# Weights prepared once for two pairs of token blocks, two of four sums kept in PSUM, and the float64 conversion in the room of a used input

## Chip, cores and metric

One NeuronCore of a Trainium2 chip runs the whole program. The metric is the time of one execution on the device in microseconds (us); of several timed runs the median counts.

## What is computed

Three layers follow one another on 2304 tokens:

```python
# 1: linear attention, 4 batches x 8 heads, 576 tokens, head width 64
proj = x @ w_phi                                  # 64 -> 128 features, for q and for k
proj = proj - max(abs(proj))
phi = concat(exp(proj), exp(-proj))
x = (phi(q) @ (phi(k).T @ v)) / (phi(q) @ sum(phi(k)) + 1e-6)
# 2: four experts, all used for every token, x is 2304 x 512
for e in range(4):
    out += p[:, e:e+1] * (relu(x @ w1[e]) @ w2[e])   # 512 -> 1024 -> 512
# 3: gated layer
y = (((x @ v1) * (x @ v2)) @ w3) @ w_out             # v1, v2: 512 -> 1024
```

The weights of the third layer (v1, v2, w3, w_out) arrive as float64, the rest as float32. Every matrix product of the layers 2 and 3 is made in three passes on split operands: each operand is written as a rounded high part and the low rest, and high x high, high x low and low x high are added.

## The kernel before

**Tokens and visits.** The tokens form six blocks of 384 (`TB`), used in pairs of 768 (`PW`): layer 2 sees pairs 0, 1, 2, layer 3 the same tokens as pairs 3, 4, 5. The hidden width of the four experts is cut into 16 columns of 256. A *visit* (list `visits`, L668 to L674) is one column of weights for one pair: the up-products, the relu and the down-products of that column. In order: 11 `plain` visits (columns 0 to 7 of pair 0, the products made directly, between the heads of the attention), 8 `expert` visits (columns 8 to 15 of pair 0), 16 for pair 1, then for each of 16 columns a `fold` (a part of w3 @ w_out, which makes one matrix of the two last ones) and an `expert` visit for pair 2, and 24 for layer 3: for each pair and each of 4 columns a `gate` (x @ v1) and a `gated` visit (x @ v2, the product of both, and the down-product).

**The up-products.** From the `expert` visits on they follow a Strassen-like scheme with 7 products in place of 8 (`strassen_up`, L732). It needs seven combinations of the weight quarters and seven of the input's quarters (`quarter_tasks`, L635: subtractions and splits on VectorE and ScalarE). The products go to three PSUM banks a, b, c of a pool of five (`mmb`). Three intermediate states of a are copied to SBUF by ScalarE (`out_of`, L740: tiles `s`), and VectorE adds banks to them (`plus`, L747), the sum staying in the SBUF tile. Four results come out, three in SBUF, one in bank a. `relu` (L773) turns each into h: ScalarE writes the high part, VectorE the low one.

**The down-products.** Six per visit (`down`, L783), each 6 matmuls of 512 columns into one of three other banks (`mma`); VectorE multiplies each by the token's share and adds it to its accumulator `acc` in SBUF (L812), of which one set of six serves one pair at a time.

**Weights.** Each visit prepares its own weights (`prefetch`, L684): a load of 512 KB on the queue of SyncE (SP) into a staging tile `raw` (two buffers), and then the splits and sums. `strassen_tasks` (L296): the split of 768 columns of raw (ScalarE casts, VectorE in the experts or POOL in the gates subtracts, L277), four sums of 256 columns on POOL (L311, tile `sm`), and the split of those 1024. The second weight is one cast and one subtraction of 1024 columns (POOL in experts and gates, VectorE in folds).

**float64.** [...] `nearest_tasks` (L321) reads the two halves of each number as integers: a load (`cr`), one ScalarE operation to `cf`, five on VectorE between `cf` and `ct`, and a store of the float32 result to DRAM (`near`). There are 40 halves (w_out 8, w3 16, v1 8, v2 8); each `expert` visit of pair 0 puts two of them into the work, each other one. The tiles cr, cf, ct have one buffer each, in a pool `cv` of their own.

**What sets the order.** `Prog.run` (L118) plans the program with given costs of each operation: an operation runs when its inputs are there and its tiles have room, the smallest number (turn of the visit, then order of writing) first. What comes out is the fixed order of each engine and of SP's queue. Side work (preparations, conversions, quarters) lies in a list `bg` and is written out piece by piece by `work()` after steps of the visit, the rest by `drain()`. The step `phase_c` (L971) waits for the whole attention, closes its pools and opens those of the transformed products; `phase_s` (L980) waits until the input of pair 0 (`xr0`) is used, closes it and opens `st`, the pool of the tiles s. All products of `strassen_up` wait for it (`after=start["S"]`). The inputs of the later pairs lie in a pool `xr` of two buffers.

Of the kernel before, what the change touches and what calls it, by code (L numbers as in the profile page):

```python
# [24 lines left out]
TB = 384  # L25
# [12 lines left out]
KA = 8  # L38
# [18 lines left out]


class Value:


    def __init__(self, prog, pool, shape, dt, tag, bufs, name):
        self.prog, self.args, self.key = prog, (shape, dt, tag, bufs, name), (pool, tag)
        self.tile, self.writers, self.readers, self.left, self.live = None, [], [], 0, False
# [4 lines left out]
    def __call__(self):  # L69
# [3 lines left out]
        return self.tile  # L73

# [7 lines left out]
class Prog:  # L82
# [15 lines left out]
    def op(self, eng, ns, fn, reads=(), writes=(), fills=(), after=(), prio=None, wait=0.0):  # L98
# [13 lines left out]
        o.values = list({id(v): v for v in (*reads, *writes, *fills)}.values())  # L112
# [79 lines left out]
def fused_kernel(ctx, tc, qT, kT, vt, w_phi, probs, w1, w2, v1, v2, w3T, w_out, out):  # L192
# [12 lines left out]
    pools["stage"] = ec(tc.tile_pool(name="stage", bufs=2))  # L205
# [62 lines left out]
    def gp(n):  # L268
        return n * 2.45 + 10

    def split_ops(raw, hi, lo, n, w, eng, after=()):

        e, ns = (nc.gpsimd, gp(n)) if eng == POOL else (nc.vector, dve(n))
# [8 lines left out]
    def load_piece(src, nm, reads, after, n=4):  # L282
        raw = V("stage", [128, n, 256], F32, "raw", 2, f"raw_{nm}")
# [37 lines left out]
    def nearest_tasks(src, key, i, h):  # L321

        nm = f"{key}{i}_{h}"
        raw = V("cv", [128, 512, 2], I32, "cr", 1, f"cr_{nm}")
        f = V("cv", [128, 512], F32, "cf", 1, f"cf_{nm}")
        t = V("cv", [128, 512], F32, "ct", 1, f"ct_{nm}")
# [3 lines left out]
                out=raw().rearrange("p c w -> p (c w)"), in_=src.bitcast(I32)[:, h * 1024:h * 1024 + 1024]  # L330
            ), 1 << 19, writes=[raw], after=start["C"]),
            lambda: op(ACT, act(n) + 90, lambda: nc.scalar.mul(
                f(), raw()[:, :, 1].bitcast(F32), 2.0 ** -112
            ), reads=[raw], writes=[f]),
            lambda: op(DVE, 430, lambda: v.tensor_scalar(
# [6 lines left out]
            lambda: op(DVE, 430, lambda: v.tensor_scalar(  # L342
# [3 lines left out]
                out=t(), in0=raw()[:, :, 0].bitcast(U32), scalar=2.0 ** -52, in1=t(), op0=ALU.mult, op1=ALU.mult  # L346
# [271 lines left out]

    quarters = {}

    def quarter(i, q):

        if (i, q) not in quarters:
            pool, bufs = ("xc", 7) if i % 2 else ("xs", 4) if q[0] == "B" else ("xt", 4)
            quarters[i, q] = V(pool, [128, 2, 2, TB], F32R, "q", bufs, f"x{i}_{q}")
# [42 lines left out]
    visits = [("plain", c, 0, (0,)) for c in range(EB)] + [("plain", c, 0, (1,)) for c in range(EB)]  # L668
# [385 lines left out]
```

## Time and profile before

| | us |
|---|---|
| median of 3 runs | 1436.79 (1435.93 to 1442.55) |
| the profiled execution | 1438.74 |
| its span | 1436.9 |

| engine | busy us | share of the span | instructions |
|---|---|---|---|
| TensorE matmul (PE) | 1328.6 | 92% | 6739 |
| TensorE weight load (PEld) | 1175.0 | 82% | 6739 |
| VectorE (DVE) | 1097.1 | 76% | 1553 |
| ScalarE (ACT) | 678.9 | 47% | 1266 |
| GpSimd (POOL) | 652.9 | 45% | 472 |

The busy times are sums over the whole span, and stages with different limits lie in it. Matmuls are pipelined and their ends are modelled, so a busy PE is not PE at its peak. In rows, the names are those of the program without buffer numbers: `h<-s,h` writes h from s and h. Idle time stands with what ended it.

### The profile page before, as it was taken

Reading aid. Unit: us, or ns where it says so; the run is one execution under the profiler, and the core shown is the slowest. Engines: PE = TensorE matmul, PEld = TensorE weight load, DVE = VectorE, ACT = ScalarE, POOL = GpSimd, SP = SyncE. Lnnn points to the kernel's source line nnn. Section 1 sums busy time; section 2 is a strip of 40 time slices with the busy share of each in tenths; the row PEclk is TensorE's granted clock in tenths of the full one; section 3 lists DMA queues with packets and bytes.
Section 4 is the critical chain, followed back from the end, with each engine's and each line's share of the span. In section 5 each row is a group of like instructions: output and inputs, shape, how many; then the busy total and the mean of one; then the engine's idle time right before and its main releaser. Section 6 shows DMA issues by size and latency. Waiting matters only on the chain.

```text
span 1436.9 us, 18521 instructions
## 1 busy us (share of the span) xinstructions
PE 1328.6 (92%) x6739; PEld 1175.0 (82%) x6739; DVE 1097.1 (76%) x1553; ACT 678.9 (47%) x1266; POOL 652.9 (45%) x472
## 2 busy tenths in 40 slices
PE   8889999999889888888979999998999999999998
PEld 7778888988777777777868778887888888889997
DVE  5678987979988988789887986667666475776665
ACT  5768866854333343333333443443443554454451
POOL 3333322304534435344543433534444758758780
PEclk8989999999999999999999999999999999999999
DMA  5554443223334244341443343332232312222311
GB/s 142 135 154 117 131 137 103 67 70 100 103 114 136 90 130 124 103 123 58 135 125 117 128 129 105 107 104 88 96 110 96 90 43 88 74 76 86 117 59 45
DMA packets 79372, 149.38 MB, mean 104 GB/s; under 512 B 33425, under 2 KB 37905, under 8 KB 79281
## 3 DMA queue, kind: packets, MB, share of 16 engines
q1 hardware_dynamic: 79280, 148.20, 33.6%
q8 instruction: 53, 0.87, 0.3%
q14 instruction: 39, 0.31, 0.1%
HBM read 130.72 MB, written 17.45 MB: 103 GB/s over the span
## 4 chain that ended last, share of the span: by engine, by line
PE 41%; DVE 34%; DMA 10%; issue 6%; ACT 6%; POOL 2%; SPq 0%; ACTq 0%; DVEq 0%; POOLq 0%
PE dn L789 15%; PE upa L720 10%; PE upb L720 5%; DVE acc L812 4%; DVE h L777 4%; PE psw L862 3%; DVE w_a L277 2%; PE upc L720 2%; DMA near_w<-cf_w 2%; PE kvp L485 2%; DMA rb<-rd 2%; DVE s L748 2%; DVE w_b L277 2%; DVE xsum L651 2%; PE num L574 2%
## 5 line engine op out<-in xcount | busy, mean ns | idle before, releaser
L789 PE MATMUL dn<-w_b,h 128*128 128x512 f32 x1728 | 433.7, 399 | 17.7 <-DVE acc L812 15.0
L789 PEld LDWEIGHTS dn<-w_b,h 128*128 128x128 f32 x1728 | 326.1, 191 | 86.3 <-DVE acc L812 19.7
L720 PE MATMUL upa<-x_T,w_a 128*128 128x384 f32 x1152 | 247.5, 351 | 54.9 <-ACT s L742 54.5
L720 PEld LDWEIGHTS upa<-x_T,w_a 128*128 128x128 f32 x1152 | 209.2, 194 | 80.6 <-ACT s L742 74.6
L311 POOL TENSOR_TENSOR sm_a<-raw_a 128x256 f32<-128x256 f32 x128 | 111.5, 871 | 287.9 <-DMA raw_a<-w 211.6
L812 DVE SCALAR_TENSOR_TENSOR acc<-dn,pn,acc 128x512 f32<-128x512 f32 x270 | 197.1, 743 | 42.6 <-PE dn L789 42.3
L277 POOL TENSOR_TENSOR w_a<-sm_a,w_a 128x1024 fp32r<-128x1024 f32 x64 | 163.1, 2549 | 79.1 <-ACT w_a L275 79.1
L277 POOL TENSOR_TENSOR w_b<-raw_b,w_b 128x1024 fp32r<-128x1024 f32 x52 | 132.9, 2555 | 131.5 <-ACT w_b L275 131.5
L550 POOL PARTITION_ALL_REDUCE M<-Ps x64 | 87.1, 1366 | 203.4 <-ACT Ps L547 182.1
L742 ACT COPY s<-upa 128x384 f32<-128x384 f32 x192 | 91.1, 475 | 114.7 <-PE upa L720 114.6
L775 ACT ACTIVATE h<-s 128x384 fp32r<-128x384 f32 x120 | 62.7, 523 | 157.1 <-DVE s L748 153.9
L748 DVE TENSOR_TENSOR s<-upb,s 128x384 f32<-128x384 f32 x128 | 70.7, 552 | 75.3 <-ACT s L742 47.2
L275 ACT CAST w_b<-raw_b 128x1024 fp32r<-128x1024 f32 x79 | 83.0, 1051 | 94.5 <-PE dn L789 60.1
L777 DVE SCALAR_TENSOR_TENSOR h<-s,h 128x384 fp32r<-128x384 f32 x120 | 96.1, 801 | 19.6 <-ACT h L775 19.5
L789 PE MATMUL dn<-w_b,g 128*128 128x512 f32 x432 | 106.8, 396 | 0.0
L277 DVE TENSOR_TENSOR w_a<-raw_a,w_a 128x768 fp32r<-128x768 f32 (+1 forms) x67 | 89.8, 1341 | 13.9 <-ACT w_a L275 13.8
L275 ACT CAST w_a<-raw_a 128x768 fp32r<-128x768 f32 (+1 forms) x91 | 74.8, 822 | 51.7 <-PE upb L720 32.3
L789 PEld LDWEIGHTS dn<-w_b,g 128*128 128x128 f32 x432 | 81.7, 191 | 15.3 <-DVE oacc L842 0.7
L275 ACT CAST w_a<-sm_a 128x1024 fp32r<-128x1024 f32 x64 | 66.8, 1044 | 45.8 <-POOL sm_a L311 45.7
L720 PE MATMUL upb<-x_B,w_a 128*128 128x384 f32 x384 | 82.5, 351 | 1.8 <-DVE s L748 1.4
L485 PEld LDWEIGHTS kvp<-vx,E 128*128 128x128 f32 x576 | 76.2, 205 | 9.2 <-ACT E L477 5.1
L485 PE MATMUL kvp<-vx,E 128*128 128x66 f32 (+1 forms) x576 | 78.0, 288 | 5.0 <-ACT E L477 2.5
(118 smaller groups left out, 2277.4 us busy)
## 6 DMA issues: line engine op xcount, KB each, us to landing
raw_a<-w SPq DMA_DIRECT2D x51, 512.0 KB
raw_b<-w SPq DMA_DIRECT2D x51, 512.0 KB
raw_a<-near_v SPq DMA_DIRECT2D x24, 512.0 KB
qr<-qT SPq DMA_DIRECT2D x32, 288.0 KB
cr_w<-w3T SPq DMA_DIRECT2D x16, 512.0 KB
cr_v<-v SPq DMA_DIRECT2D x16, 512.0 KB
raw_b<-near_wo SPq DMA_DIRECT2D x16, 512.0 KB
raw_b<-wfold SPq DMA_DIRECT2D x12, 512.0 KB
```

Source lines behind the costliest of these rows:

```text
L275: lambda: op(ACT, act(n), lambda: nc.scalar.copy(out=hi(), in_=raw[1]()), reads=[raw[0]], fills=[w], after=after),
L277: lambda: op(eng, ns, lambda: e.tensor_tensor(out=lo(), in0=raw[1](), in1=hi().bitcast(F32), op=ALU.subtract), reads=[raw[0], w], fills=[w ...
L311: ops.append(lambda k=k, out_=out_, a=a, b=b, how=how: op(eng, ns, lambda: e.tensor_tensor(out=out_(), in0=a(), in1=b(), op=how), reads=[r ...
L485: nc.tensor.matmul(kvp()[:, a].rearrange("p h d -> p (h d)") if rest else kvp()[:, a, h], E()[:, a] if rest else E()[:, t, a, h], w()[:, 4 ...
L550: op(POOL, 1171, lambda M=M, Ps=Ps: nc.gpsimd.partition_all_reduce(M(), Ps(), channels=128, reduce_op=bass_isa.ReduceOp.absmax), reads=[Ps ...
L720: nc.tensor.matmul(ps(), w()[:, a, i, kk * 128:kk * 128 + 128], x()[:, j, kk], start=first and n == 0, stop=last and n == total - 1, skip_ ...
L742: op(ACT, act(TB, False), lambda: nc.scalar.copy(out=t(), in_=ps()), reads=[ps], writes=[t], after=start["S"])
L748: op(DVE, dve(TB), lambda: nc.vector.tensor_tensor(out=t(), in0=ps(), in1=t(), op=ALU.add), reads=[ps], writes=[t])
L775: op(ACT, act(TB, sbuf), lambda: nc.scalar.activation(out=h()[:, 0], in_=src(), func=AF.Relu), reads=[src], fills=[h])
L777: op(DVE, dve(TB), lambda: nc.vector.scalar_tensor_tensor(out=h()[:, 1], in0=src(), scalar=0.0, in1=h()[:, 0].bitcast(F32), op0=ALU.max, o ...
L789: nc.tensor.matmul(ps(), hs[fc]()[:, x, t * 128:(t + 1) * 128], w()[:, fc * 2:fc * 2 + 2, y], start=fc == 0 and n == 0, stop=fc == 1 and n ...
L812: op(DVE, dve(DM), lambda a=a, ps=ps, share=share: nc.vector.scalar_tensor_tensor(out=a(), in0=ps(), scalar=share(), in1=a(), op0=ALU.mult ...
```

## The change

- The list of visits is new: the columns 8 to 15 are visited once for the pairs 1 and 0 (in this order), then, with folds ahead of each, columns 0 to 7 once for the pairs 1 and 2, and 8 to 15 for pair 2 alone; in layer 3 one visit `gates` does both up-products, for the pairs 3 and 4 together and then for pair 5.
- Two sets of accumulators (`acc`, `acc2`) serve the two pairs.
- In the experts all of `strassen_tasks` now subtracts on POOL.
- Of the four results, two sums are written back into the bank they came from (`stay`), in the experts and in the second up-product of the gates; the first up-product of the gates keeps all four in SBUF.
- The conversion uses the room of an input that has been read: a tile of the pool `xr` is cut into two raw parts, f and t (`near_room`, class `Part`). Three halves are put into the work per double visit, 20 in columns 8 to 15 and 20 in the columns 0 to 7.
- `raw` has three buffers, `st` seven (it opens with `phase_c`, so the products wait for `start["C"]`; the first sum of an accumulator of `acc2` waits for `phase_s`). The quarters T2 to T4 of even pairs lie in a pool of three, the others in one of four. The quarters of pair 1 are written out ahead of those of pair 0; those of later pairs after the up-products of the pair ahead.
- The planner's costs of POOL, of two VectorE shifts and of VectorE's splits are higher.

```diff
-    pools["stage"] = ec(tc.tile_pool(name="stage", bufs=2))
+    pools["stage"] = ec(tc.tile_pool(name="stage", bufs=3))
...
     def gp(n):
-        return n * 2.45 + 10
+        return n * 2.3 + 200
+
+    def beside(n):
+        return dve(n) * (BESIDE if "C" in start else 1)
...
-    def nearest_tasks(src, key, i, h):
+    def nearest_tasks(src, key, i, h, room):
 
         nm = f"{key}{i}_{h}"
-        raw = V("cv", [128, 512, 2], I32, "cr", 1, f"cr_{nm}")
-        f = V("cv", [128, 512], F32, "cf", 1, f"cf_{nm}")
-        t = V("cv", [128, 512], F32, "ct", 1, f"ct_{nm}")
+        raw, f, t = room[h], room[2], room[3]
...
+    def near_room(i):
+
+        r = V("xr", [128, 4, PW], F32, "x", 2, f"near{i}")
+        flat = lambda a, b: lambda x: x.rearrange("p k t -> p (k t)")[:, a:b]
+        return [Part(r, lambda x, h=h: flat(h * 1024, h * 1024 + 1024)(x).bitcast(I32)) for h in range(2)] + [
+            Part(r, flat(2048 + h * 512, 2560 + h * 512)) for h in range(2)
+        ]
...
-    visits += [("plain", c, 0, (0, 1)) for c in range(EB, KA)]
-    visits += [("expert", c, 0, None) for c in range(KA, NE * NQ)]
-    visits += [("expert", c, 1, None) for c in range(NE * NQ)]
+    visits += [("plain", c, (0,), (0, 1)) for c in range(EB, KA)]
+    visits += [("expert", c, (1, 0), None) for c in range(KA, NE * NQ)]
     for c in range(NE * NQ):
-        visits += [("fold", c, None, None), ("expert", c, 2, None)]
-    visits += [(k, c, i, None) for i in range(3, 6) for c in range(NQ) for k in ("gate", "gated")]
+        visits += [("fold", c, (), None), ("expert", c, (1, 2) if c < KA else (2,), None)]
+    visits += [("gates", c, x, None) for x in ((3, 4), (5,)) for c in range(NQ)]
...
-            made.append(strassen_tasks(src1, f"a{v}", first=DVE) if kind == "expert" else split_tasks(
-                src1, "ring1", f"a{v}", after=after))
+            made.append(split_tasks(src1, "ring1", f"a{v}", after=after) if kind == "plain" else strassen_tasks(src1, f"a{v}"))
...
-            t = V("st", [128, TB], F32, "s", 9, f"s{n}_{nm}")
+            t = V("st", [128, TB], F32, "s", 7, f"s{n}_{nm}")
...
-        def plus(t, ps):
-            op(DVE, dve(TB), lambda: nc.vector.tensor_tensor(out=t(), in0=ps(), in1=t(), op=ALU.add),
-               reads=[ps], writes=[t])
+        def plus(t, ps, stay):
+            to = ps if stay else t
+            op(DVE, dve(TB), lambda: nc.vector.tensor_tensor(out=to(), in0=ps(), in1=t(), op=ALU.add),
+               reads=[t if stay else ps], writes=[to])
             work()
+            return to, not stay
...
-        plus(s1, c)
-        yield (0, 0), s1, True
+        yield (0, 0), *plus(s1, c, stay)
...
-        plus(s3, b)
-        yield (1, 1), s3, True
+        yield (1, 1), *plus(s3, b, False)
...
-        plus(s2, b)
-        yield (0, 1), s2, True
+        yield (0, 1), *plus(s2, b, stay)
...
-            if c == 0:
-                sums[i, t, g] = V("acc", [128, DM], F32, "acc", 6, f"acc{i}_{t}{g}")
+            if c == first[i]:
+                sums[i, t, g] = V(("acc", "acc2")[i % 2], [128, DM], F32, "acc", 6, f"acc{i}_{t}{g}")
...
                     start["C"] = [op("HOST", 1, phase_c, after=attention)]
+                    prefetch(v + 1)
+                    bg.extend(quarter_tasks(1))
                     bg.extend(quarter_tasks(0))
...
+            for i in pairs:
+                turn += 1
+                pg.base = EXPERTS * turn
+                nm, h = f"{v}_{i}", {}
+                if kind == "expert":
+                    for _ in range(0 if len(pairs) < 2 else 1 + (i == 1)):
+                        if len(near_todo) > (20 if c >= KA else 0):
...
+                            bg.extend(nearest_tasks(srcs[k][n], k, n, half, rooms[z]))
+                    for ft, src, sbuf in strassen_up(wa[v], i, nm, True):
+                        h[ft] = relu(src, sbuf, f"{nm}_{ft[0]}{ft[1]}")
...
+                bg.extend(later)
+                for d in behind:
+                    d()
+                if later:
+                    drain()
+                later = quarter_tasks(i + 2) if c == last[i] and i < 4 and i != 0 else []
...
-        open_pool("cv", bufs=1, side="right")
         open_pool("sm", bufs=1, side="right")
-        open_pool("xt", bufs=4, side="right")
+        open_pool("xt", bufs=3, side="right")
         open_pool("xc", bufs=7, side="right")
+        open_pool("st", bufs=7, side="right")
 
     def phase_s():
         close_pool("xr0")
-        open_pool("st", bufs=9)
+        open_pool("acc2", bufs=6)
```

## Rows read from the trace of the kernel before

**Rows 1.** The page, first line: the length of the profiled execution's span.

```profile
span 1436.9 us, 18521 instructions
```

**Rows 2.** Busy time by stage: engines' busy us with (x instructions), granted TensorE clock, DMA.

```profile
345.00:510.00 165.00, 143.52 (x671) 124.60 (x670) 144.04 (x189) 64.67 (x106) 73.08 (x53) 0.96 0.35 112
510.00:830.00 320.00, 282.20 (x1315) 245.21 (x1315) 272.39 (x364) 123.03 (x206) 140.71 (x94) 0.95 0.37 115
830.00:1134.00 304.00, 292.30 (x1402) 253.88 (x1401) 210.62 (x269) 130.21 (x206) 132.10 (x94) 0.99 0.32 104
1134.00:1437.00 303.00, 288.24 (x1462) 263.29 (x1460) 192.97 (x244) 132.59 (x222) 204.49 (x149) 0.98 0.23 74
```

**Rows 3.** Timeline of TensorE in the untransformed stage: start, length, instruction.

```profile
318.38 4.35 PE L720 MATMUL up<-x_B,w_a 128*128 128x384 f32 x24
322.57 4.34 PE L789 MATMUL dn<-w_b,h 128*128 128x512 f32 x18
326.75 4.35 PE L720 MATMUL up<-x_B,w_a 128*128 128x384 f32 x24
```

**Rows 4.** VectorE's groups from 345 to 830: busy us, mean ns | idle before, releaser.

```profile
L812 DVE SCALAR_TENSOR_TENSOR acc<-dn,pn,acc 128x512 f32<-128x512 f32 x141 | 102.9, 742 | 11.0 <-PE dn L789 10.8
L777 DVE SCALAR_TENSOR_TENSOR h<-s,h 128x384 fp32r<-128x384 f32 x75 | 66.0, 881 | 7.3 <-ACT h L775 7.2
L277 DVE TENSOR_TENSOR w_a<-raw_a,w_a 128x768 fp32r<-128x768 f32 x24 | 31.2, 1299 | 0.8 <-ACT w_a L275 0.8
L748 DVE TENSOR_TENSOR s<-upb,s 128x384 f32<-128x384 f32 x50 | 27.6, 552 | 14.5 <-ACT s L742 10.9 <-PE upb L720 3.5
L338 DVE SCALAR_TENSOR_TENSOR cf_w<-cf_w,ct_w 128x512 int32<-128x512 int32 x16 | 16.7, 1041 | 0.2
...
L777 DVE SCALAR_TENSOR_TENSOR h<-upa,h 128x384 fp32r<-128x384 f32 x25 | 13.6, 546 | 0.0
L348 DVE TENSOR_TENSOR cf_w<-cf_w,ct_w 128x512 f32<-128x512 f32 x16 | 13.6, 851 | 0.1
...
L335 DVE TENSOR_SCALAR ct_w<-cf_w 128x512 int32<-128x512 int32 x16 | 13.0, 810 | 18.8 <-ACT cf_w L332 18.8
...
L277 DVE TENSOR_TENSOR x_T<-xsum,x_T 128x768 fp32r<-128x768 f32 x8 | 7.6, 952 | 0.9 <-ACT x_T L275 0.9
```

**Rows 5.** VectorE on tiles h and cf_w, whole span: min/median/max ns, first, last.

```profile
L777 DVE SCALAR_TENSOR_TENSOR h<-s,h x120: 543/558/2567, 352.2 to 1125.3; 128x384 fp32r<-128x384 f32 x120
L777 DVE SCALAR_TENSOR_TENSOR h<-upa,h x40: 541/546/558, 357.9 to 1123.6; 128x384 fp32r<-128x384 f32 x40
...
L335 DVE TENSOR_SCALAR ct_w<-cf_w x16: 410/428/2168, 445.1 to 630.6; 128x512 int32<-128x512 int32 x16
L338 DVE SCALAR_TENSOR_TENSOR cf_w<-cf_w,ct_w x16: 675/788/2417, 446.1 to 631.2; 128x512 int32<-128x512 int32 x16
```

**Rows 6.** Timeline of all engines around 580 us: start, length, instruction [idle before].

```profile
575.98 0.67 ACT L332 ACTIVATE cf_w<-cr_w 128x512 f32<-128x512 f32 x1
576.16 2.40 POOL L277 TENSOR_TENSOR w_b<-raw_b,w_b 128x1024 fp32r<-128x1024 f32 x1 [1.22 <-ACT w_b L275]
...
576.68 2.16 DVE L335 TENSOR_SCALAR ct_w<-cf_w 128x512 int32<-128x512 int32 x1 [0.26 <-ACT cf_w L332]
...
589.22 0.67 ACT L332 ACTIVATE cf_w<-cr_w 128x512 f32<-128x512 f32 x1 [4.77 <-DMA near_w<-cf_w]
```

**Rows 7.** POOL's groups from 1134 to 1437, columns as in rows 4.

```profile
L277 POOL TENSOR_TENSOR w_a<-raw_a,w_a 128x768 fp32r<-128x768 f32 x22 | 43.0, 1955 | 42.8 <-ACT w_a L275 42.8
```

**Rows 8.** VectorE's groups from 830 to 1134, columns as in rows 4.

```profile
L277 DVE TENSOR_TENSOR w_a<-raw_a,w_a 128x512 fp32r<-128x512 f32 x14 | 23.7, 1694 | 7.7 <-ACT w_a L275 7.7
L277 DVE TENSOR_TENSOR w_b<-raw_b,w_b 128x1024 fp32r<-128x1024 f32 x15 | 23.7, 1579 | 2.9 <-ACT w_b L275 2.5 <-POOL sm_a L311 0.4
```

**Rows 9.** TensorE's waits from 345 to 830: us in total, times, longest.

```profile
PE upa L720 <- ACT s L742: 39.2, 24, 3.9
PE dn L789 <- DVE acc L812: 14.7, 10, 2.7
```

More of the change, by code (lines that the diff above doesn't have):

```diff
@@ L111, in op @@
         o.deps.discard(o)
-        o.values = list({id(v): v for v in (*reads, *writes, *fills)}.values())
+        o.values = list({id(v.root): v.root for v in (*reads, *writes, *fills)}.values())
         for v in o.values:
@@ L282, in load_piece @@
     def load_piece(src, nm, reads, after, n=4):
[L283 removed]
+        raw = V("stage", [128, n, 256], F32, "raw", 3, f"raw_{nm}")
         return raw, [lambda: dma(
@@ L701, in prefetch @@
         else:
-            n = near["v1" if kind == "gate" else "v2", c]
-            made.append(strassen_tasks(lambda: n(), f"a{v}", reads=[n]))
-            if kind == "gated":
-                made.append(split_tasks(lambda: wfold[c](), "ring2", f"b{v}", reads=[wfold[c]], eng=POOL))
+            n1, n2 = near["v1", c], near["v2", c]
+            made.append(strassen_tasks(lambda: n1(), f"a{v}", reads=[n1]))
+            made.append(split_tasks(lambda: wfold[c](), "ring2", f"b{v}", reads=[wfold[c]], eng=POOL))
+            made.append(strassen_tasks(lambda: n2(), f"g{v}", reads=[n2]))
         plan(made)
-        wa[v] = made[0][0]
-        if len(made) > 1:
-            wb[v] = made[1][0]
+        wa[v], wb[v] = made[0][0], made[1][0]
+        if len(made) > 2:
+            wg[v] = made[2][0]
     def bank(width, name, pool="mma"):
@@ L882, in run_visits @@
         drain()
-        gates = {}
-        for v, (kind, c, i, blocks) in enumerate(visits):
+        rooms, later = [None, None], []
+        for v, (kind, c, pairs, blocks) in enumerate(visits):
             drain()
@@ L891, in run_visits @@
                     start["S"] = [op("HOST", 1, phase_s, after=raws[0].readers + raws[0].writers)]
-                prefetch(v + 1)
-            if kind == "expert":
-                for _ in range(2 if i == 0 else 1):
-                    if near_todo:
-                        k, n, h = near_todo.popleft()
-                        bg.extend(nearest_tasks(srcs[k][n], k, n, h))
-                if c == 8 and i is not None and kind == "expert":
-                    bg.extend(quarter_tasks(i + 1))
-            if kind == "gate" and c == 1 and i < 5:
-                bg.extend(quarter_tasks(i + 1))
-            now = []
+                else:
+                    if c == 0 and pairs == (1, 2):
+                        later = quarter_tasks(2)
+                    prefetch(v + 1)
+            if kind == "fold":
+                fold(v, c)
+                continue
             if kind == "plain":
@@ L909, in run_visits @@
                         d()
[L910 removed]
+                    behind = [lambda v=v, c=c, t=t, hs=hs: expert_down(v, 0, c, t, hs)]
                 continue
[L912 to L943 removed]
```

109 lines of the change are left out of this document (54 added, 55 removed).

## The prediction, made before the change was run

> **What bounds the kernel now.** All sums here are made against the profiled execution, 1438.7 us, of which the span is 1436.9 [rows 1]. The median of the three timed runs, 1436.8, lies 1.9 us lower; I take those 1.9 off at the end. A difference under about 0.5% (7 us) could not be told from no change.
>
> I read the stage table first [rows 2], with stages cut where the kind of visit changes: 345 us (pair 0's transformed visits), 510 (pair 1), 830 (folds with pair 2), 1134 (gated half). Then I ask what TensorE alone would need. In the untransformed stage it runs without gaps [rows 3]: 24 matmuls of 384 columns from 318.38 to 322.57, so 1.047 us for six; 18 of 512 columns from 322.57 to 326.75, so 1.39 us for six. A transformed visit has 7 groups of the first and 6 of the second kind: 7 x 1.047 + 6 x 1.39 = 15.7 us, and a fold (12 of 512 columns) 2.8 us.
>
> Against that, the 24 visits from 345 to 830 take 485 us, 20.2 each. That is 4.5 us per visit, 108 us in all, above TensorE's need. From 830 on a visit with its fold takes 304/16 = 19.0 us against 18.5, so 2.7% over. The table shows the difference in the DVE column: 144.0 of 165 and 272.4 of 320 us are busy (416.4 of 485, 0.859), but only 0.69 and 0.64 in the last two stages, where TensorE is close to its need. So **VectorE bounds the 485 us from 345 to 830**, and TensorE the rest. The granted clock, 0.95 to 0.96 there against 0.98 to 0.99 after, is a consequence: TensorE slows after its waits.
>
> Then I read what VectorE does in that stretch [rows 4], and how far each operation is from its own minimum [rows 5]. The operations with one input in PSUM keep to their time: h<-upa is 541 to 558 ns. Those with both inputs in SBUF do not: h<-s is 543 at least but 881 in the mean of this stretch, with a maximum of 2567; the conversion's first shift is 410 at least and 810 in the mean. The timeline shows what holds them [rows 6]: at 576.68 a shift takes 2.16 us beside a POOL subtraction that started at 576.16 and ran 2.40. POOL is busy 213.8 of the 485 us (0.44) [rows 2].
>
> **The change part by part.**
>
> *Fewer preparations.* Expert visits go from 40 to 24 (8 for pairs 1 and 0, 8 for pairs 1 and 2, 8 for pair 2), gate columns from 12 to 8. That drops 24 transformed preparations (two per gate column) and 20 splits of second weights, with 44 loads of 512 KB on SP. POOL now spends 213.8/24 = 8.9 us per preparation; with the 768-column subtraction, which moves from VectorE to it at 1.96 us [rows 7], 10.9. That serves two pairs, some 34 us, so POOL's share falls from 0.44 to 0.32. VectorE loses the 1.30 us of w_a per visit [rows 4]. The saved ACT and POOL time is worth nothing directly, since neither bounds; it counts through VectorE's stalls. The dropped loads count nothing: SP queues far less than it could, and its conversion loads and stores are as many as before.
>
> *Two of four sums kept in banks.* The relu then reads PSUM for three of four results. Per pair and visit VectorE needs 3 x 0.546 + 0.881 = 2.52 us for h, 3 x 0.552 = 1.66 for the additions (one input in PSUM as before; that the output goes to PSUM I take at no cost, bounded below by 0 and above by the 0.3 us by which h<-s exceeds h<-upa), 6 x 0.742 = 4.45 for acc: 8.63. No row shows PSUM dearer than SBUF: the minima are 541 and 543 [rows 5]. [...]
>
> *Conversions.* 40 halves before and after, five VectorE instructions each: 2 x 0.810 + 1.041 + 2 x 0.851 = 4.36 us now [rows 4], 2 x 0.41 + 3 x 0.675 = 2.85 undisturbed [rows 5]. I scale the excess, 1.51, by POOL's share: 2.85 + 1.51 x 0.32/0.44 = 3.95, with ends 2.85 and 4.36. They spread over 16 + 16 pair visits, 1.25 each, where it was 1.67 in 24.
>
> *Stage A', columns 8 to 15 for pairs 1 and 0 (16 pair visits).* VectorE: 8.63 + 1.25 x 3.95 = 4.94, and the rest of the two inputs' quarters after 345 (9 operations of 0.952 [rows 4] over 16 visits: 0.5): 14.1 us, now below TensorE's 15.7. Two engines so close do not hide each other's waits. If the stage keeps VectorE's busy share of today, a pair takes 14.1/0.859 = 16.4. If instead VectorE's idle time of today (20.2 - 17.35 = 2.9 us a visit, much of it before a conversion's first shift, which waits for ACT [rows 4]) comes on top of TensorE's need, in proportion to the conversions, 15.7 + 2.9 x 1.25/1.67 = 17.9. No row says which, so I take the middle, 17.1: 274 us. Ends: 258 (15.7 with the 2.7% of the last stages) and 297 (15.7 + 2.9).
>
> *Stage B', folds with pairs 1 and 2 (8 visits).* 2 x 8.63 + the fold's two splits 1.69 + 1.58 [rows 8] + 2.5 x 3.95 + two inputs' quarters (22 x 0.952/8 = 2.6) = 33.0; over 0.859, 38.4 us; TensorE's way, 2 x 15.7 + 2.8 + 2 x 2.2 = 38.6. So 307 us; ends 281 (34.2 with 2.7%) and 319 (34.2 + 2 x 2.9).
>
> *Stage C', folds with pair 2 alone (8 visits).* As now, 19.0 each: 152; it loses a 1.1 us split from VectorE, which does not bound there.
>
> Sum 733 against 789 (345 to 1134): 56 less.
>
> *Moved work at 345.* Pair 1's quarters (11 VectorE operations) now come ahead of pair 0's rest (8); the same 19 stood close together before, and the untransformed visits cover most. What is late next is the first product of pair 1: plus 3 us, from 0 to 6. The new waits: the first acc of pair 1 waits for the release of pair 0's input, and acc's of the visits behind it queue on VectorE; that release comes with the quarters, well before, at nothing. The conversions' first load waits until pair 1's input is used; the load queues on SP ahead of weight loads, which a third staging buffer now covers. From 0 to 345 the work is the same: 0, give or take 2.
>
> *Gated half.* 303 us against 12 x (14 x 1.047 + 6 x 1.39) = 276 plus the tail of the pair before: TensorE-bound. Halved preparations for pairs 3 and 4 take away some of the waits: minus 3, from 0 to minus 10.
>
> Together 56 - 3 + 3 = 56: 1438.7 - 56 = 1382.7, on the scale of the median **1381 us**.
>
> **Rivals.**
>
> *TensorE's floor.* If POOL's lighter load ends the stalls (lower ends: 258 + 281 + 152 = 691, 98 less, gates minus 10, no loss at 345), the time is 1329. For it: undisturbed, VectorE needs only 12.4 us for a pair in A'. Against: the POOL subtractions stay as long, and each still holds one VectorE operation.
>
> *The conversion's own chain sets the pace.* One f tile serves all halves. ACT starts one at 575.98 and the next only at 589.22, after waiting 4.77 us for the store of the first [rows 6]: 13.2 us a half. In order on ACT, the copies of upa stand behind that wait, and TensorE behind them: 39.2 us, the longest of its waits [rows 9]. The change keeps one f and asks three halves per double visit: 20 x 13.2 = 264 us for 7 visits, in A' and again in B', plus one visit each (32 and 36): 596 + 152 = 748, that is 41 less, 1396. Against: the shifts wait only 18.8 us in all for ACT in the 16 halves of w3 [rows 4], and with a second raw tile a load no longer waits for the half before.
>
> *It does not do what it says.* The dropped preparations are hidden anyway (POOL idles over half of the time), and the 108 us come from conversions alone, 2.7 a half, which all stay: only the gates' 3 us are left, 1434.
>
> *The kept sums hold the banks too long (slower).* Two of the five banks now stay taken through ACT's relu and VectorE's h, where the addition freed them before. A product that finds no bank stops TensorE, and the copies behind it. The price is the queueing of one more step on each engine; at 2 us for each of 52 transformed up-projections (40 in experts, 12 gated) 104 us, 1485. It decides from (1444 - 1381)/52 = 1.2 us each. For it: [rows 9] show TensorE already waiting 14.7 us on acc, that is for banks. Against: those are the other three banks, and a pair's next two products have free ones.
>
> **How the numbers follow.** Forecast 0.48; conversion chain 0.24; floor 0.12; no change 0.08; banks 0.08. Faster by over 0.5% is the first three, 0.84; within it 0.08; slower 0.08. The range begins at the floor, 1329. The upper ends all at once (297 + 319 + 152 = 768, plus 6 at 345, nothing from the gates) would be 1422; I close it at 1410, which takes in the chain (1396) with one of the two upper ends. Left out are the last two rivals, 0.16.
>
> **What would show it.** Right: VectorE's busy share from 345 still above 0.8, POOL's near 0.32, h from PSUM at 0.55, a pair in A' at 16.4 to 17.9 us, double visits with folds near 38.5, single ones unchanged at 19. The floor: 16.1 and 35 us, and VectorE's share below 0.8. The chain: ACT's waits for the near stores grow over today's, and upa waits behind them. Wrong altogether: TensorE waiting for VectorE's or ACT's h before a product gets a bank; conversions as slow as before though POOL's share fell.

## The result, and the profile after

| | before | changed |
|---|---|---|
| median, us | 1436.36 | 1338.77 |
| runs | 4 (1429.2 to 1442.55) | 4 (1336.39 to 1339.86) |
| span of the profiled execution, us | 1436.9 | 1334.6 |

The ratio of the runs is 0.932, with a 95% interval of 0.9275 to 0.9365. The change makes the kernel 97.6 us faster. The forecast was 1381 us, the range 1329 to 1410; the time lies in it, but 10 us from the case called TensorE's floor (1329) and 42 from the forecast. In two of the experiments below one execution of four took far longer than the rest (2116 and 3270 us), so their medians are those of the other three.

The first lines of the page of the changed kernel:

```profile
span 1334.6 us, 18054 instructions
## 1 busy us (share of the span) xinstructions
PE 1286.8 (96%) x6739; PEld 1154.1 (86%) x6739; DVE 972.0 (73%) x1513; ACT 614.4 (46%) x1198; POOL 478.3 (36%) x348
```

TensorE has the same 6739 matmuls, but 124 instructions of POOL and 40 of VectorE are gone. The stages of the changed kernel, cut at its own visits (0 to 338.6, A' to 602.6, B' to 883.3, C' and the gates behind), with the columns of rows 2:

```profile
338.60:602.60 264.00, 252.45 (x1232) 223.94 (x1231) 213.46 (x321) 91.36 (x163) 81.12 (x54) 0.99 0.29 90
602.60:883.30 280.70, 272.66 (x1351) 242.46 (x1350) 227.04 (x338) 110.45 (x193) 79.29 (x56) 1.00 0.35 112
883.30:1049.80 166.50, 164.41 (x811) 144.50 (x810) 100.67 (x132) 71.58 (x118) 87.92 (x61) 1.00 0.30 98
1049.80:1334.60 284.80, 278.32 (x1453) 258.46 (x1451) 162.36 (x242) 114.43 (x201) 128.30 (x96) 1.00 0.16 52
```

A pair in A' takes 264/16 = 16.5 us and a double visit with its fold 280.7/8 = 35.1. They are to be set beside the stages of the kernel before, cut at the same places in its work: the first and the ninth fold, and the first product of the gates. The first fold starts at 809.7 there, not at 830:

```profile
809.70 0.39 PE L862 MATMUL psw<-w_b,w_a 128*128 128x512 f32 x1
971.89 2.88 PE L862 MATMUL psw<-w_b,w_a 128*128 128x512 f32 x12
1134.61 1.22 PE L720 MATMUL upa<-x_B,w_a 128*128 128x384 f32 x6
```

```profile
345.00:809.70 464.70, 407.24 (x1892) 354.43 (x1891) 399.09 (x530) 178.33 (x295) 205.64 (x140) 0.95 0.36 112
809.70:971.90 162.20, 154.55 (x752) 133.74 (x751) 118.95 (x154) 69.20 (x112) 65.51 (x45) 1.00 0.35 115
971.90:1134.60 162.70, 156.83 (x745) 136.02 (x744) 109.19 (x139) 70.77 (x111) 75.25 (x56) 0.98 0.31 99
1134.60:1436.90 302.30, 287.64 (x1459) 262.80 (x1457) 192.79 (x243) 132.21 (x221) 203.97 (x148) 0.98 0.23 74
```

So the 24 visits without a fold took 464.7/24 = 19.4 us each, and a visit with its fold 162.2/8 = 20.3, where the cut at 830 in [rows 2] gives 20.2 and 19.0. The work of A' and B' took 626.9 us before (345 to 971.9) and takes 544.7 now: 82 of the 102 us by which the span is shorter. 6 more lie ahead of 338.6 (it was 345), and 14 behind: C' takes 166.5 in place of 162.7, the gates 284.8 in place of 302.3. (In the kernel before, 2.6 us of the experts' last down-products lie in the gates, now none.) The granted clock from 338.6 to 883.3 is 0.99 where it was 0.95 in the 24 visits, VectorE's busy share 440.5/544.7 = 0.81 (399.1/464.7 = 0.86 in the 24 visits), POOL's 160.4/544.7 = 0.29.

VectorE's groups in that stretch, columns as in rows 4, and below them TensorE's waits there, columns as in rows 9:

```profile
L833 DVE SCALAR_TENSOR_TENSOR acc<-dn,pn,acc 128x512 f32<-128x512 f32 x175 | 128.7, 744 | 27.8 <-PE dn L810 27.0
L361 DVE TENSOR_TENSOR near<-near 128x512 f32<-128x512 f32 x40 | 41.2, 1030 | 0.3
L358 DVE SCALAR_TENSOR_TENSOR near<-near 128x512 f32<-128x512 uint32 x40 | 33.8, 844 | 0.2
L351 DVE SCALAR_TENSOR_TENSOR near<-near 128x512 int32<-128x512 int32 x40 | 30.6, 765 | 0.2
L355 DVE TENSOR_SCALAR near<-near 128x512 int32<-128x512 int32 x40 | 27.3, 683 | 0.3
L798 DVE SCALAR_TENSOR_TENSOR h<-s,h 128x384 fp32r<-128x384 f32 x32 | 22.1, 690 | 0.6 <-ACT h L796 0.6
L348 DVE TENSOR_SCALAR near<-near 128x512 int32<-128x512 int32 x40 | 19.4, 485 | 30.5 <-ACT near L345 30.5
...
L771 DVE TENSOR_TENSOR upc<-upc,s 128x384 f32<-128x384 f32 x32 | 17.9, 558 | 7.3 <-PE upc L741 7.1
L798 DVE SCALAR_TENSOR_TENSOR h<-upc,h 128x384 fp32r<-128x384 f32 x32 | 17.8, 555 | 7.1 <-ACT h L796 7.1
L771 DVE TENSOR_TENSOR s<-upb,s 128x384 f32<-128x384 f32 x32 | 17.7, 553 | 8.4 <-ACT s L764 8.2
```

```profile
PE upa L741 <- ACT s L764: 15.6, 16, 2.2
PE dn L810 <- DVE acc L833: 3.6, 4, 1.5
PE upb L741 <- DVE s L771: 0.2, 1, 0.2
```

A conversion costs VectorE 0.485 + 0.765 + 0.683 + 0.844 + 1.030 = 3.81 us where [rows 4] gave 4.36 for the halves of w3, h<-s 0.69 in place of 0.88, and the h of kept sums 0.55. TensorE waits 19.4 us for named causes; the two lines of [rows 9] add up to 53.9. No row shows it waiting for an h before a product can have a bank.

### The profile page after: what moved, and what is told of

The parts are those of the page before. It is cut to its first block, busy times and chain, and to the rows that moved or that the text cites. A ratio compares the mean times of both kernels' runs of the same rounds, so it can differ in the third digit from the quotient of the medians.

```text
span 1334.6 us, 18054 instructions
## 1 busy us (share of the span) xinstructions
PE 1286.8 (96%) x6739; PEld 1154.1 (86%) x6739; DVE 972.0 (73%) x1513; ACT 614.4 (46%) x1198; POOL 478.3 (36%) x348
## 4 chain that ended last, share of the span: by engine, by line
PE 62%; DVE 16%; DMA 11%; ACT 5%; issue 4%; POOL 1%; SPq 1%; ACTq 0%; POOLq 0%; DVEq 0%
PE dn L810 25%; PE upa L741 8%; PE upb L741 4%; PE kvp L498 3%; PE psw L883 2%; DMA rb<-rd 2%; DVE acc L833 2%; PE num L587 2%; DMA near_v<-near 2%; PE upc L741 2%; PE up L741 2%; DVE near L361 2%; DMA near_wo<-near 2%; DMA rd<-d 1%; PE upa_3b L741 1%
## 5 line engine op out<-in xcount | busy, mean ns | idle before, releaser
L741 PE MATMUL upa<-x_T,w_a 128*128 128x384 f32 x720 | 148.7, 341 | 16.2 <-ACT s L764 16.1
L292 POOL TENSOR_TENSOR w_b<-raw_b,w_b 128x1024 fp32r<-128x1024 f32 x32 | 80.2, 2507 | 227.1 <-ACT w_b L290 227.1
L741 PEld LDWEIGHTS upa<-x_T,w_a 128*128 128x128 f32 x720 | 127.7, 189 | 29.8 <-ACT s L764 24.7
L292 POOL TENSOR_TENSOR w_a<-raw_a,w_a 128x768 fp32r<-128x768 f32 x32 | 61.4, 1917 | 233.7 <-ACT w_a L290 233.6
L326 POOL TENSOR_TENSOR sm_a<-raw_a 128x256 f32<-128x256 f32 x64 | 52.5, 821 | 141.0 <-DMA raw_a<-w 60.6
L292 POOL TENSOR_TENSOR w_a<-sm_a,w_a 128x1024 fp32r<-128x1024 f32 x32 | 80.3, 2511 | 10.6 <-ACT w_a L290 10.6
L587 PE MATMUL num<-Eq,KV 128*128 128x288 f32 x328 | 71.9, 348 | 6.9 <-ACT Eq L571 2.7
L741 PE MATMUL up<-x_B,w_a 128*128 128x384 f32 x384 | 71.7, 337 | 0.0
L741 PEld LDWEIGHTS up<-x_B,w_a 128*128 128x128 f32 x384 | 66.7, 188 | 0.6
L587 PEld LDWEIGHTS num<-Eq,KV 128*128 128x128 f32 x328 | 51.7, 191 | 15.8 <-ACT Eq L571 3.8
L571 ACT ACTIVATE Eq<-Ps 128x288 f32<-128x288 f32 x128 | 50.7, 444 | 22.0 <-DVE Ps L566 20.3
```

Source lines behind the costliest of these rows:

```text
L292: lambda: op(eng, ns, lambda: e.tensor_tensor(out=lo(), in0=raw[1](), in1=hi().bitcast(F32), op=ALU.subtract), reads=[raw[0], w], fills=[w ...
L326: ops.append(lambda k=k, out_=out_, a=a, b=b, how=how: op(eng, ns, lambda: e.tensor_tensor(out=out_(), in0=a(), in1=b(), op=how), reads=[r ...
L571: op(ACT, act(HS), lambda a=a, E=E, Ps=Ps: nc.scalar.activation(out=E()[:, a], in_=Ps(), func=AF.Exp, scale=1.0 - 2 * a), reads=[Ps], fill ...
L587: nc.tensor.matmul(num(), KV[i]()[:, a, 2 * h:2 * h + 2].rearrange("p c d -> p (c d)"), EE[j]()[:, a], start=n == 0, stop=n == len(parts) - 1)
L741: nc.tensor.matmul(ps(), w()[:, a, i, kk * 128:kk * 128 + 128], x()[:, j, kk], start=first and n == 0, stop=last and n == total - 1, skip_ ...
```

## The experiments

Each was timed beside the kernel before on its chip (medians 1433.8 to 1436.2 us there); the numbers in brackets behind a time are its ratio to that kernel and the 95% interval, to be held against 0.9275 to 0.9365 for the changed kernel. Theory A was that VectorE's work, made longer by POOL's subtractions, had set the pace from 345 to 830; B that the conversions' own chain (load, ScalarE, VectorE, store) had; C that the new costs in the plan had done it.

### The preparations made for each pair again

```diff
-    visits += [("expert", c, (1, 0), None) for c in range(KA, NE * NQ)]
+    visits += [("expert", c, (i,), None) for c in range(KA, NE * NQ) for i in (1, 0)]
...
-        visits += [("fold", c, (), None), ("expert", c, (1, 2) if c < KA else (2,), None)]
+        visits += [("fold", c, (), None)] + [("expert", c, (i,), None) for i in ((1, 2) if c < KA else (2,))]
...
-    visits += [("gates", c, x, None) for x in ((3, 4), (5,)) for c in range(NQ)]
+    visits += [("gates", c, (i,), None) for x in ((3, 4), (5,)) for c in range(NQ) for i in x]
```

> The changed kernel, but each pair of a double visit prepares its weights for itself (16 expert columns and 4 gate columns twice more); order of the products, kept sums, conversions in the input's room and planner costs stay. Theory A (VectorE's time, swollen by POOL's subtractions, had set the pace; sharing the preparations took POOL off it): POOL's share from 340 to 885 us goes from 0.30 to over 0.5, a conversion from 3.8 us of VectorE to 4.5 or more, a pair from 16.5 us to 18 or more, the time to 1370 to 1400 us. Theory B (the conversions' pace set it, and spreading them over 32 pair visits in place of 24, with a second raw tile, is what helped): under 1350 us. Theory C (the new costs in the plan did it): under 1350 us.

Measured: 1401.33 us (0.978, 0.9729 to 0.9831). The same stretch, from the first transformed product to the first fold of C':

```profile
343.30:934.50 591.20, 543.08 (x2620) 475.41 (x2619) 481.43 (x661) 246.22 (x407) 324.48 (x216) 0.98 0.38 121
```

POOL is busy 324.5/591.2 = 0.55, and the stretch is 46.5 us longer than in the changed kernel. In that view of this kernel, the five operations of a conversion take 0.753 + 0.861 + 1.005 + 1.074 + 1.050 = 4.74 us. The result is a little over what A allowed (1370 to 1400) and far from B and C. So sharing the preparations is worth 1401.3 - 1338.8 = 63 us, two thirds of the gain, and the other edits together make the rest (1434.4 - 1401.3 = 33). Of the 66 us by which the span is longer than the changed kernel's, 13.7 lie in the gates, which take 298.5 us here (1102.5 to 1401).

### POOL's long subtractions made twice

A preparation given back brings casts, loads and ring buffers with it. This run adds work on POOL alone: the same result again.

```diff
             ), reads=[raw[0], w], fills=[w], after=after),
-        ]
+        ] + ([lambda: op(eng, ns, lambda: e.tensor_tensor(
+                out=lo(), in0=raw[1](), in1=hi().bitcast(F32), op=ALU.subtract
+            ), reads=[raw[0], w], fills=[w], after=after)] if eng == POOL and n == 1024 else [])
```

> The changed kernel with every 1024-column subtraction on POOL made twice (the same result again); nothing else is added, no cast, no load. Theory A: POOL's share from 340 to 885 us goes from 0.30 to about 0.45, as before the change; a conversion takes 4.3 us of VectorE or more, h<-s 0.85, and the time goes to 1350 to 1370 us. If the stalls are hidden now that VectorE has slack: VectorE's operations longer as said, but under 1345 us. Theories B and C: under 1345 us, and VectorE's operations as they are.

Measured: 1416.45 us (0.9879, 0.9831 to 0.9927), much more than A allowed. By stages (up to C', C', gates):

```profile
344.00:919.20 575.20, 534.93 (x2591) 471.73 (x2590) 473.90 (x663) 202.19 (x357) 232.09 (x136) 0.98 0.30 97
919.20:1094.20 175.00, 167.76 (x804) 144.25 (x803) 106.99 (x131) 70.78 (x118) 140.59 (x82) 0.99 0.29 94
1094.20:1416.00 321.80, 292.62 (x1453) 266.86 (x1452) 174.43 (x242) 114.60 (x201) 181.38 (x117) 0.96 0.15 46
```

The first stretch is what the run was for: 575.2 against 544.7, 30.5 us, with POOL's share at 0.40 and a conversion at 0.792 + 1.228 + 0.666 + 0.858 + 1.018 = 4.56 us. That agrees with A; h<-s does not, which was expected at 0.85 and takes 0.64, less than the 0.69 of the changed kernel. That the weights come later could be another cause. It is not here: in this stretch neither TensorE's nor ScalarE's list of waits has a line for POOL. What grows is a chain, ScalarE's wait for VectorE's sums and TensorE's for ScalarE's copies s. ScalarE's longest wait of that kind in the changed kernel, and in this run with TensorE's wait below it:

```profile
ACT h L796 <- DVE upc L771: 54.3, 21, 6.2
```

```profile
ACT h L798 <- DVE upc L773: 66.5, 23, 6.1
...
PE upa L743 <- ACT s L766: 29.6, 21, 3.0
```

ScalarE's waits for all three sums add up to 82.4 us in the changed kernel and 113.1 here, TensorE's wait for s to 15.6 and 29.6. The rest of the 81 us lies ahead of 344 (5), in C' (8.5) and above all in the gates (37), where TensorE has waits that it does not have in the changed kernel, among them 5.5 us for POOL's weights and 7.3 for g; that part the expectation had left out. The waits for POOL are late weights; how the 37 us divide is not shown.

Set beside each other, the three kernels grow in the same order, though not in proportion:

| kernel | POOL's share | a conversion on VectorE, us | A' and B', us |
|---|---|---|---|
| changed | 0.29 | 3.81 | 544.7 |
| POOL's subtractions twice | 0.40 | 4.56 | 575.2 |
| prepared for each pair | 0.55 | 4.74 | 591.2 |

VectorE's busy share is 0.81, 0.82 and 0.81 in them, with 659, 663 and 661 instructions: what grows is not its share but the length of single operations, and ScalarE and TensorE wait behind those.

### The conversions' VectorE work left out of the kernel before

This kernel leaves out the five VectorE operations of each conversion, so the last layer's weights are not those of the reference; load, ScalarE's operation and store stay.

```diff
-            lambda: op(DVE, 430, lambda: v.tensor_scalar(
-                out=t().bitcast(I32), in0=f().bitcast(I32), scalar1=3, scalar2=None, op0=ALU.logical_shift_left
-            ), reads=[f], writes=[t]),
...
-            lambda: op(DVE, dve(n), lambda: v.tensor_tensor(
-                out=f(), in0=f(), in1=t(), op=ALU.add
-            ), reads=[t], writes=[f]),
```

> The kernel before, leaving out the five VectorE operations of each conversion (the load, the ScalarE operation and the store stay, so the weights of the last layer are not the reference's). Theory A (VectorE's load, with POOL's stalls, costs the 108 us that TensorE loses from 345 to 830): VectorE gets 17.4 - 1.67 x 4.4 = 10 us a visit, the 24 visits fall to 16.2 us each, and the time to 1335 to 1350 us. Theory B (the conversions' chain of load, ScalarE and store sets the pace): the waits for the stores stay, and the time is over 1400 us.

Measured: 1356.4 us (0.9437, 0.9392 to 0.9482), 77 us less than the 1433.8 beside it, 6 us above A's end, and far from B. The 24 visits, in the columns of rows 2:

```profile
340.00:729.30 389.30, 379.50 (x1892) 341.39 (x1891) 251.64 (x358) 180.77 (x297) 197.86 (x141) 1.00 0.44 136
```

They take 389.3/24 = 16.2 us each, as expected, at a granted clock of 1.00, although POOL is busy 0.51 of the time and ScalarE still waits for the stores. The time is 6 us over the range because the stretch began from 464.7 us and not from 485: it loses 75 us, and 88 was all that it had above TensorE's need. ScalarE's longest wait in the kernel before (345 to 809.7), and below it the waits of this run (340 to 729.3):

```profile
ACT h L775 <- DVE s L748: 111.4, 48, 7.0
```

```profile
ACT h L759 <- DVE s L732: 47.4, 37, 2.8
...
ACT cf_w L332 <- DMA near_w<-cf_w: 19.1, 10, 4.6
ACT cf_v L332 <- DMA near_v<-cf_v: 11.0, 8, 3.3
...
PE upa L704 <- ACT s L726: 9.5, 8, 3.0
```

VectorE's operations are still stretched (h<-s takes 0.77 us, the 768-column split 1.10), so POOL's share of 0.51 costs next to nothing when VectorE has room. The stalls cost time where VectorE is near its limit: with 0.65 of the stretch busy it has room for them, with 0.86 it had not. The run shortens the conversions' chain too, since f goes straight on to its store; what that chain is worth by itself is seen from the second f below, 13 us of this stretch.

### Parts by themselves, in the kernel before

Two of four sums of the experts kept in banks:

```diff
-        def plus(t, ps):
+        def plus(t, ps, stay):
+            to = ps if stay else t
...
```

> The kernel before with two of four sums of the experts kept in their banks, nothing else. Here POOL is busy 0.44 of the stretch from 345 to 830 and h<-s takes 0.88 us against 0.55 from a bank. Theory A: two of these per visit become 0.55, 0.67 us a visit of VectorE, over the busy share of 0.86 some 0.8 us for 24 visits: 15 to 25 us less, 1410 to 1420. If the additions or the banks give it back: 1430 or more. In the changed kernel the same edit was worth about 5 us.

Measured: 1413.37 us (0.9836, 0.9816 to 0.9857), 22.8 us less than the 1436.2 beside it, as theory A had it.

The planner's costs of the change (POOL, shifts, splits):

```diff
-        return n * 2.45 + 10
+        return n * 2.3 + 200
...
-        e, ns = (nc.gpsimd, gp(n)) if eng == POOL else (nc.vector, dve(n))
+        e, ns = (nc.gpsimd, gp(n)) if eng == POOL else (nc.vector, dve(n) * (1.3 if "C" in start else 1))
...
-            lambda: op(DVE, 430, lambda: v.tensor_scalar(
+            lambda: op(DVE, 700, lambda: v.tensor_scalar(
...
```

> The kernel before with nothing new but the planner's costs of the change (POOL 2.3 ns per column plus 200, shifts 700, VectorE's splits times 1.3). In the changed kernel these costs were worth some 15 us. Theory A (VectorE has more to do than TensorE in the stretch from 345 to 830, whatever the order): 1430 to 1440 us. If the order of the plan is worth the same here: 1415 to 1425 us.

Measured: 1424.55 us (0.9922, 0.9889 to 0.9954), 9 us less: A's expectation failed by 5 us, and the time lies at the end of the range in which the order of the plan counts as much here. In the profile the 24 visits fall by 24 us (table below) with the same work, so VectorE's load by itself does not fix the length of the stretch.

A second buffer for f:

```diff
-        f = V("cv", [128, 512], F32, "cf", 1, f"cf_{nm}")
+        f = V("cv", [128, 512], F32, "cf", 2, f"cf_{nm}")
...
```

> The kernel before with two buffers of the tile f of the conversions (and, for the room, eight s tiles in place of nine and a small table in another pool), so that ScalarE no longer waits there for the store of the conversion before (36 us of its waits between 345 and 830). Theory A (VectorE has more to do than TensorE): TensorE's wait for the copies s (39 us) turns into waits for VectorE, and the time falls by 0 to 10 us, 1425 to 1435. Theory B (the conversions' chain sets the pace): 20 us less or more, under 1415.

Measured: 1420.07 us (0.9885, 0.9855 to 0.9915), 16 us less, between the two expectations. ScalarE's waits for the near stores are gone from its list, yet TensorE's waits in the 24 visits (343.4 to 795.2) are nearly those of [rows 9]:

```profile
PE upa L720 <- ACT s L742: 34.4, 22, 3.2
PE dn L789 <- DVE acc L812: 16.0, 10, 2.7
```

The granted clock of that stretch is 0.98 in place of 0.95, and 9.5 of the 13 us that it loses are TensorE's busy time (397.8 us in place of 407.2). The chain is thus a part of the loss, but not its pace.

The 24 visits of the kernel before, from the first transformed product to the first fold, with each part by itself:

| kernel | 24 visits, us | VectorE's busy share | granted clock |
|---|---|---|---|
| before | 464.7 | 0.86 | 0.95 |
| a second f | 451.8 | 0.91 | 0.98 |
| two sums kept in banks | 447.6 | 0.85 | 0.97 |
| the planner's costs | 440.9 | 0.88 | 0.97 |
| conversions' VectorE work left out | 389.3 | 0.65 | 1.00 |

### Parts taken back from the changed kernel

The planner's costs of before:

```diff
-BESIDE = 1.3
+BESIDE = 1.0
...
-        return n * 2.3 + 200
+        return n * 2.45 + 10
...
-            lambda: op(DVE, 700, lambda: v.tensor_scalar(
+            lambda: op(DVE, 430, lambda: v.tensor_scalar(
...
```

> The changed kernel with the planner's costs of before (POOL 2.45 ns per column plus 10, shifts 430 ns, splits on VectorE without the factor 1.3). Theory A and theory B: the work is the same, 1336 to 1348 us. Theory C (the plan's order did it): 1365 us or more.

Measured: 1353.4 us (0.944, 0.9391 to 0.9489): 15 us more, above what A and B allowed and below C. TensorE's wait for acc from 341 to 896 is 9.3 us in place of 3.6. The costs are a part of the gain of their own.

All sums to SBUF:

```diff
-                    for ft, src, sbuf in strassen_up(wa[v], i, nm, True):
+                    for ft, src, sbuf in strassen_up(wa[v], i, nm, False):
...
```

> The changed kernel, but all sums of the up-products go to SBUF as before, so that three of four results are read from SBUF by the relu. Theory A: two more operations per pair and visit are exposed to POOL, about 0.15 us each at POOL's share of today (h<-s takes 0.69 against 0.55 us), and VectorE is no longer the bound: plus 0 to 12 us, 1339 to 1351. If banks held longer cost TensorE something: faster than the changed kernel, under 1334 us.

Measured: 1343.86 us (0.9389, 0.9332 to 0.9445), 5 us more, inside A's expectation; its interval overlaps that of the changed kernel, so the 5 us are not clear of the spread of the runs. h<-s takes 0.70 us there, as one of four does in the changed kernel.

The experts' 768-column subtraction on VectorE:

```diff
-            made.append(split_tasks(src1, "ring1", f"a{v}", after=after) if kind == "plain" else strassen_tasks(src1, f"a{v}"))
+            made.append(split_tasks(src1, "ring1", f"a{v}", after=after) if kind == "plain" else strassen_tasks(src1, f"a{v}", first=DVE))
```

> The changed kernel with the 768-column subtraction of the experts' weights on VectorE again, where it was before, 24 of them. VectorE gets 0.95 us or a little more per double visit, POOL loses 1.96 us of some 33, a share of 0.24 in place of 0.30. Theory A (POOL's share sets how long VectorE's operations are): the two nearly cancel, conversions get shorter (under 3.7 us), and the time is 1333 to 1344 us. If the move itself was worth what its VectorE time says (24 x 1.3 us before): 1350 us or more.

Measured: 1339.32 us (0.9306, 0.9247 to 0.9365): no difference that can be told, as A had it. What was expected of the conversions is not shown, since of this run only times are used.

### A version faster than both

The changed kernel keeps one f for all halves, and ScalarE waits before the next one until the store has landed:

```profile
ACT near L345 <- DMA near_v<-near: 18.6, 12, 4.0
...
ACT near L345 <- DMA near_wo<-near: 16.4, 8, 4.8
...
ACT near L345 <- DMA near_w<-near: 15.4, 10, 2.9
```

Written into the raw part that the numbers came from, of which there are two, the result leaves f free at once:

```diff
-                out=f(), in0=f(), in1=t(), op=ALU.add
-            ), reads=[t], writes=[f]),
+                out=raw()[:, :n].bitcast(F32), in0=f(), in1=t(), op=ALU.add
+            ), reads=[f, t], writes=[raw]),
...
```

> The changed kernel with the result of a conversion written into the raw part it came from, which has two copies, and stored from there, so that the next conversion's first operation on ScalarE no longer waits for the store (50 us of ScalarE's waits between 340 and 885). The load after next waits for the store instead. If those waits still held TensorE: 5 to 15 us less, 1324 to 1334 us, and TensorE's wait for the copies s (15.6 us) falls below 8. If ScalarE's waits lie in slack: 1336 to 1341 us.

Measured: 1327.18 us (0.9226, 0.9174 to 0.9278), in the range given for the case that those waits still held TensorE; the interval just touches that of the changed kernel. TensorE's waits from 344 to 874.5:

```profile
PE upa L741 <- ACT s L764: 5.2, 11, 0.7
PE dn L810 <- DVE acc L829: 3.0, 1, 3.0
```

The wait for the copies s falls from 15.6 to 5.2 us, and the stretch (343.9 to 874.5) from 544.7 to 530.6. With VectorE's load off the path, the conversions' chain was the next wait in line.

With the 768-column subtraction back on VectorE as well:

```diff
...
-            made.append(split_tasks(src1, "ring1", f"a{v}", after=after) if kind == "plain" else strassen_tasks(src1, f"a{v}"))
+            made.append(split_tasks(src1, "ring1", f"a{v}", after=after) if kind == "plain" else strassen_tasks(src1, f"a{v}", first=DVE))
```

> The changed kernel with the conversion's result stored from its raw part (11 us less by itself) and the experts' 768-column subtraction on VectorE again (no difference by itself). Theory A: the two do not touch each other, 1323 to 1331 us; POOL's share falls to 0.24 from 340 to 880 us and conversions take 3.6 us of VectorE in place of 3.8. If VectorE is again close to its limit with 0.95 us more per double visit: over 1333 us.

Measured: 1325.81 us (0.9226, 0.9194 to 0.9257). No difference to the run above can be told, but the interval lies wholly below that of the changed kernel. In its stretch (343.4 to 876) POOL's share is 130.4/532.6 = 0.24, and a conversion takes 0.572 + 0.734 + 0.559 + 0.823 + 0.923 = 3.61 us, as expected.

## Why the prediction was right, and where it was off

**The bound.** VectorE's load sets the pace of the 24 visits from 345: shown. Without the conversions' VectorE work they run at 16.2 us, near TensorE's 15.7. But it is no fixed limit: the planner's order alone gives 24 us back.

**Fewer preparations.** That they count through VectorE's stalls: shown, by POOL's work alone (30.5 us for 0.11 more of its share) and by preparing twice (46.5 us in the same stretch). POOL's share was forecast at 0.32 and is 0.29; a conversion at 3.95 us and is 3.81.

**Kept sums.** h from a bank takes 0.545 to 0.555 us and the addition into it 0.558 to 0.562, against 0.553 into SBUF. That PSUM is taken at no cost was right within 10 ns. Kept sums are worth 23 us in the kernel before and 5, not clear of the spread, in the changed one, probably because the same stalls can be saved only once; no run shows that reason.

**The term that was off** is the sum for A' and B', 274 + 307 = 581 us, which measured 544.7. Three steps of it failed. The first is the division by 0.859: 14.1 and 33.0 are sums of mean durations, 0.859 is a share of busy time, and these are not the same measure, since VectorE's operations overlap their successors in the profile. In the changed kernel:

```profile
400.29 2.14 DVE L355 TENSOR_SCALAR near<-near 128x512 int32<-128x512 int32 x1
402.36 0.54 DVE L798 SCALAR_TENSOR_TENSOR h<-upb,h 128x384 fp32r<-128x384 f32 x1
```

The second starts at 402.36, before the first ends at 402.43. The 21 groups from 338.6 to 883.3 add up to 477.5 us, in 440.5 us of busy time: 8% too much. Nor is 0.859 a ceiling: the table of the 24 visits has 0.91 in a shorter time. The second step is the size of the durations in B'. They add up to 30.7 us a double visit, not 33.0: a conversion takes 3.47 us there, not 3.95 (4.14 in A'), and h<-s 0.72 (0.66 in A'), where the text scaled the conversions by POOL's share but left h<-s at 0.881. In busy time a pair in A' needs 213.5/16 = 13.3 us and a double visit in B' 227.0/8 = 28.4. At a share of 0.859 that would be 15.5 and 33.0, under TensorE's 15.7 and 34.2. The third is "on top of TensorE's need", today's 2.9 us of VectorE's idle time scaled by the conversions: TensorE lost 0.8 us a pair in A' and 0.9 a double visit in B', not 2.2 a pair. Waits that come from VectorE's lateness went with the lateness and were no sum of their own. That a pair in A' measured 16.5, beside the 16.4 of the first step, is luck: it is TensorE's 15.7 and its 0.8 of waits.

**TensorE's floor** came near in time (the range begins there), but not for the reason given. The stalls did not end: a conversion takes 3.81 us against 2.85 undisturbed, h<-s 0.69 against 0.54. VectorE, busy 0.81, had room for them: TensorE lost 0.8 us a pair.

**The cut at 830** is a misreading: the first fold starts at 809.7. So the 24 visits were 3.7 us each above TensorE's need, 88 us in all, and not 4.5 and 108. VectorE's share is 0.86 with either cut, so the reading of the bound stands. But a visit with its fold took 20.3 us, not 19.0, and C', forecast at 152, took 166.5, 14.5 more.

**The gated half** was forecast to lose 3 us, at most 10, and lost 17.5 (302.3 to 284.8), some 15 of them without the down-products that moved out of it. The reason given, the halved preparations, fits; the size does not. TensorE's listed waits there fell from 10.3 us to 2.6 and its granted clock rose from 0.98 to 1.00; with the preparations made for each pair again it takes 298.5. That C' and the gates miss by nearly the same amount in opposite ways is luck, too. Against the profile the forecast is off by 46 us: 36 in A' and B', 15 in the gates and 9 at 345 the one way, 14.5 in C' the other.

**Left out** was what the planner's costs are worth: they stand in the change, and the text gave them no term. Taken back they cost 15 us.

**At 345** the first transformed product came 6.4 us earlier, where the text had 3 us later. Why is not shown: other versions of the changed kernel start it between 338.3 and 344.2. **Banks**: no wait for a kept one is in the trace, and the sums back in SBUF are not faster; the 2 us for each that this rival reckoned with was the author's assumption and stood on no row. **The chain** did not set the pace, but some 11 us of it were left.

## What to carry to other kernels

Where POOL and VectorE work side by side on SBUF, POOL's idle time does not say that its work is free (here 0.11 more of POOL's share, from 0.29 to 0.40, made the stage 30.5 us longer): look at the minimum and the mean of those VectorE operations that read nothing from PSUM, and count POOL's work by what it adds to them. It mattered here with VectorE busy 0.81 to 0.86 of a stretch, and hardly with 0.65, where POOL's share of 0.51 went with 16.2 us a visit, 0.5 above TensorE's need. A sum of durations is set against a sum of durations, busy time against busy time (the two were 8% apart here); where two engines come out within a tenth of each other, that decides which one bounds. And a stage is cut at the first instruction of its work, looked up in the timeline: a cut 20 us late made one stage too long here and the next too short.

## What was not expected of the hardware

Work on POOL that touches nothing VectorE writes made a stage 30.5 us longer, with VectorE's busy share nearly unchanged (0.82 against 0.81). Means of the h that read a bank stayed at 0.545 to 0.556 us at POOL shares from 0.24 to 0.55, while a conversion went from 3.61 to 4.74. Single groups do not follow POOL's share alone: h<-s took 0.69 us at a share of 0.29, 0.64 at 0.40, 0.88 at 0.44 and 0.77 at 0.51. The conversions' shifts, which read one tile and that from SBUF, are stretched like the operations with two inputs there: the second one takes 409 to 2512 ns in the changed kernel. TensorE was slower after some of its waits, not after all. In the kernel before, six matmuls took 1.22 us with no wait ahead of them, 2.29 after one of 3.90 us, and 1.31 after one of 2.26:

```profile
405.94 2.29 PE L720 MATMUL upa<-x_T,w_a 128*128 128x384 f32 x6 [3.90 <-ACT s L742]
...
574.83 1.22 PE L720 MATMUL upa<-x_B,w_a 128*128 128x384 f32 x6
...
721.02 1.31 PE L720 MATMUL upa<-x_T,w_a 128*128 128x384 f32 x6 [2.26 <-ACT s L742]
```

TensorE's granted clock does not follow the sum of its waits: with a second f the named waits of the stretch are nearly the same, and the clock is 0.98 in place of 0.95. The longest wait does not order the runs either (up to 3.9 us at 0.95 in the kernel before, 5.4 at 0.97 with the planner's costs, 4.7 at 0.98 with the preparations made for each pair). What sets it stays open.
